# Attention with a forgetting decay, then a gated FFN, on one core: rows of q and k filled by DMA instead of cleaned on GpSimd, other load times, and a last output summed piece by piece

## The chip, the cores and the metric

The kernel runs on one core of one Trainium2 chip. The metric is the time of one execution in microseconds (us) as the device measures it. The engines are named as in the profile: PE is TensorE's matmul, PEld its weight load, DVE is VectorE, ACT is ScalarE, POOL is GpSimd, and SP is SyncE, which in this kernel only issues DMAs.

## The reference

Two stages, one behind the other. The first is causal attention whose scores carry a decay from a running sum over log f; the second is an FFN with a convolution over three neighbours and a gate. There are 8 batches, 8 heads, 576 positions, a head width of 64, 512 model columns and 1024 FFN columns.

```
scores = scale * np.matmul(q, k.transpose(0, 1, 3, 2))
log_f = np.log(np.clip(f, 0.0001, 1.0))
cum = np.cumsum(log_f, axis=-1)
decay = cum[:, :, :, None] - cum[:, :, None, :]
scores = np.where(causal, -1000000000.0, scores + decay)
attn = softmax(scores)
x = heads side by side of np.matmul(attn, v)
...
h = np.maximum(x @ w_in, 0.0)
conv_out += conv_w[k][None, None, :] * hp[:, k:k + S, :]   # k = 0, 1, 2
gate = 1.0 / (1.0 + np.exp(-conv_out))
return h * gate @ w_out
```

## The kernel before

A **half batch** (hb, 0 to 15) is four heads of one batch; a **block** (b, 0 to 7) is one batch, so two half batches and then the FFN of their 576 rows.

q and k are loaded by transposing DMAs (`load_qk`, four ring buffers `stq` and `stk`) that see the 64 float32 of a head as 128 16-bit columns. Afterwards the odd partitions of a buffer hold the upper halves, which are used as bfloat16, and the even partitions hold the lower halves, which are of no use. `clamp` therefore multiplies the even partitions by zero and sets a constant there where it is needed (two instructions for each side of a half batch, 1152 columns each). `rows_of` then overwrites one even row of q and two of k with the cumulated log f (in DRAM as `kd`), so that the score matmul adds the decay by itself. For half batch 0 the decay comes from extra matmuls on `sel_k` and `sel_q`.

The scores of a half batch come in groups: the tail (the last 64 positions), the diagonal tiles and the tiles off the diagonal. ACT takes their exponentials; POOL zeroes what lies above the diagonal in the diagonal tiles and the tail (`diag_mask`, `tail_mask`, by affine_select). When a block's eight heads are there, PE sums the columns (`sums`), DVE turns and inverts the sums (`recip`, L376 and L377, once in a block) and spreads them (`spread`, L380), PE multiplies by v (`pv`), and DVE scales the result into `xt` (`norm`, L389).

The FFN of a block has eight pieces (ff) of 128 columns: `ffn1` on PE, `relu` on ACT, two scalar_tensor_tensor on DVE for the convolution (L409, L411), `tanh` on ACT, and one more on DVE for the gate (L418), into `hg`. Only when all eight are there does `ffn2` run, for five row groups of the output, each with one chain of eight matmuls over ff; ACT copies the result out and SP stores it.

What stands where on an engine is decided by a list scheduler in plain Python (`Plan`): each task has engines with a cost, predecessors, a key and buffers that it takes and gives. The order that comes out is the order in each engine's queue; at run time each engine works through its own queue and waits only for semaphores. Before the change the clamps of half batches 1 and 2 may go to POOL or DVE, all later ones go to POOL, and `rows_of` is issued from POOL:

```
cl.append(add({"POOL": 1.35, "DVE": 0.6} if hb < 3 else {"POOL": 1.35}, [t_ld[hb, s]], base - 1.0 + 0.1 * (2 * p + s),
...
t_rows[hb] = add({"POOL": 1.1}, cl, base - 0.8, lambda me, hb=hb: rows_of(hb), lag=2.5)
```

v comes as float32 by SP and is cast to float16 by POOL or DVE (L224, L226); the weights are loaded with a cast by DMAs from POOL.

## Time and profile before

| | |
|---|---|
| three runs | 332.43, 333.64 and 336.59 us; median 333.64 us |
| the profiled execution | 335.01 us, its span 333.3 us |
| mean granted TensorE clock | 0.923 |
| busy in the span | PE 78%, DVE 84%, ACT 60%, POOL 55% |

The span runs from the first instruction to the last; 1.7 us of the profiled execution lie outside it. A busy share is a mean over stages: the first third waits for loads, the last fifth has no loads left. A DVE or POOL instruction counts as busy from its start to its end, however much of that it stood still.

### The profile page before, as it was taken

How to read it: one execution, taken by the hardware profiler on the slowest of the kernel's cores; microseconds unless marked ns; L12 is line 12 of the kernel's file. 1: busy time of each engine (PE TensorE's matmuls, PEld its weight loads, DVE VectorE, ACT ScalarE, POOL GpSimd, SP SyncE). 2: the span in 40 equal slices, each digit the busy share in tenths (PEclk: the TensorE clock that was granted, in tenths of full speed). 3: DMA queues.
4: the chain of work that ended last, by engine and by line, in shares of the span. 5: the costliest groups of instructions: out<-in, count | busy, mean ns of one | idle time of the engine just before them, and what ended most of it. 6: DMA issues, size and time to landing. Idle time of an engine off the chain costs nothing.

```text
span 333.3 us, 6984 instructions
## 1 busy us (share of the span) xinstructions
PE 259.6 (78%) x2832; PEld 177.3 (53%) x2832; DVE 279.2 (84%) x319; ACT 201.0 (60%) x267; POOL 184.8 (55%) x193
## 2 busy tenths in 40 slices
...
GB/s 174 232 195 194 196 198 195 197 133 221 220 177 104 94 218 96 120 65 223 149 140 63 83 177 181 2 65 151 73 4 63 76 9 63 66 18 0 128 16 142
DMA packets 126182, 40.97 MB, mean 123 GB/s; under 512 B 118693, under 2 KB 121893, under 8 KB 126150
## 3 DMA queue, kind: packets, MB, share of 16 engines
q1 hardware_dynamic: 118592, 37.76, 53.3%
...
q10 hardware_dynamic: 326, 0.45, 0.5%
...
q14 instruction: 10, 0.08, 0.1%
...
## 4 chain that ended last, share of the span: by engine, by line
DVE 38%; PE 35%; SPq 11%; issue 5%; DMA 4%; ACT 4%; POOL 2%; DVEq 0%; POOLq 0%; ACTq 0%
PE ps L425 13%; DVE hg L418 10%; DVE u L409 9%; PE ps L399 9%; SPq L196 8%; DVE u L411 8%; PE ps L366 7%; PE ps L305 5%; DVE va L224 3%; DMA vf<-in_v_dram 3%; DVE xt L389 3%; SPq L218 3%; DVE rb L380 2%; DVE va L226 1%; DMA stk<-kd 1%
## 5 line engine op out<-in xcount | busy, mean ns | idle before, releaser
L305 PE MATMUL ps<-stq,stk 128*128 128x128 bf16 (+3 forms) x576 | 64.7, 254 | 31.5 <-DVE stq L202 10.6
L399 PE MATMUL ps<-xt,w_in_f 128*128 128x288 f16 x512 | 77.5, 303 | 13.3 <-ACT ht L403 8.5
L414 ACT ACTIVATE hg<-u,cw 128x576 f16<-128x576 f32 x64 | 49.5, 776 | 62.2 <-DVE u L411 62.0
L425 PE MATMUL ps<-w_out_f,hg 128*128 128x512 f16 x256 | 66.7, 415 | 21.0 <-DVE hg L418 17.3
L418 DVE SCALAR_TENSOR_TENSOR hg<-hg,ht 128x576 f16<-128x576 f16 x64 | 67.1, 1057 | 9.1 <-ACT hg L414 8.9
L332 ACT ACTIVATE pp<-ps 128x1024 f16<-128x1024 f32 x64 | 64.1, 1022 | 12.2 <-PE ps L305 10.1
L409 DVE SCALAR_TENSOR_TENSOR u<-ht,cwt 128x576 f32<-128x576 f16 x64 | 67.5, 1066 | 4.4 <-ACT ht L403 4.4
L399 PEld LDWEIGHTS <-w_in_f 128*128 128x128 f16 x512 | 51.6, 103 | 33.6 <-issue 14.7
L411 DVE SCALAR_TENSOR_TENSOR u<-ht,cwt,u 128x576 f32<-128x576 f16 x64 | 65.7, 1037 | 0.8
L305 PEld LDWEIGHTS <-stk 128*128 128x128 bf16 x576 | 41.5, 104 | 44.3 <-issue 12.6
L345 POOL TENSOR_SCALAR_AFFINE_SELECT pp<-pd 128x1024 f16<-128x1024 f32 x32 | 39.6, 1236 | 33.8 <-ACT pd L342 33.1
L425 PEld LDWEIGHTS <-hg 128*128 128x128 f16 x256 | 26.3, 105 | 55.2 <-DVE hg L418 20.0
L202 POOL TENSOR_SCALAR stk<-stk,lim 128x1152 uint16<-128x1152 uint16 x29 | 50.5, 1744 | 0.5 <-DMA stk<-in_k_dram 0.5
L202 POOL TENSOR_SCALAR stq<-stq,lim 128x1152 uint16<-128x1152 uint16 x28 | 46.1, 1646 | 4.9 <-DMA stq<-in_q_dram 2.8
L403 ACT ACTIVATE ht<-ps 128x576 f16<-128x576 f32 x64 | 41.0, 651 | 12.4 <-PE ps L399 12.1
L320 POOL TENSOR_SCALAR_AFFINE_SELECT pt<-p 128x256 f16<-128x256 f32 x16 | 11.0, 689 | 60.1 <-ACT p L317 60.1
L342 ACT ACTIVATE pd<-ps 128x1024 f32<-128x1024 f32 x32 | 32.7, 1023 | 3.8 <-PE ps L305 2.1
L366 PE MATMUL ps<-pp,ones_h 128*64 128x128 f16 (+3 forms) x576 | 28.6, 249 | 1.0 <-POOL pp L345 0.6
L438 ACT COPY ob<-ps 128x1024 f32<-128x1024 f32 (+1 forms) x24 | 19.1, 796 | 14.7 <-PE ps L425 13.5
L366 PEld LDWEIGHTS <-ones_h 128*64 128x64 f16 x640 | 24.0, 116 | 7.0 <-issue 4.3
L366 PE MATMUL ps<-pp,va 128*64 128x128 f16 (+3 forms) x576 | 25.5, 241 | 2.6 <-DVE xt L389 2.6
L366 PEld LDWEIGHTS <-va 128*64 128x64 f16 x640 | 22.6, 111 | 6.7 <-issue 4.8
...
## 6 DMA issues: line engine op xcount, KB each, us to landing
...
stq<-in_q_dram SPq DMA_TRANSPOSE x17, 5.9
```

Of the source, the lines that this page charges most:

```text
L202: eng.tensor_scalar(t, t, lim[:, 2 * side:2 * side + 1], lim[:, 2 * side + 1:2 * side + 2], op0=ALU.mult, op1=ALU.add)
L305: nc.tensor.matmul(o, tk[:, h * S + k0:h * S + k0 + 128], tq[:, h * S + q0:h * S + q0 + n], start=True, stop=hb > 0)
L332: nc.scalar.activation(pp_t[slot[t_dg, "p"]][:, 1024 * s:1024 * (s + 1)], ps_t[slot[t_sc, "ps"]], AF.Exp, scale=SCALE)
L345: nc.gpsimd.affine_select(pp_t[slot[t_dg, "p"]][:, 2048:3072].rearrange("p (m j) -> p m j", j=128), pd_t[slot[t_ex, "pd"]].rearrange("p (m ...
L366: nc.tensor.matmul(ps[64 * s:64 * (s + 1), AB + q0:AB + q0 + n], left_of(s, h, m), p, start=first and x in (0, 3), stop=last and x in (2, ...
L399: nc.tensor.matmul(ps[:, MB + 288 * a:MB + 288 * (a + 1)], w_in_f16[:, cc, 128 * ff:128 * (ff + 1)], xt[:, cc, 288 * a:288 * (a + 1)], sta ...
L403: nc.scalar.activation(ht_t[slot[t_m1, "ht"]][:, 1:1 + S], ps_t[slot[t_m1, "ps"]][:, MB:MB + S], AF.Relu, scale=0.5)
L409: nc.vector.scalar_tensor_tensor(u, ht[:, 0:S], cwt[:, ff, 0:1], ht[:, 1:1 + S], op0=ALU.mult, op1=ALU.add)
L411: nc.vector.scalar_tensor_tensor(u, ht[:, 2:2 + S], cwt[:, ff, 1:2], u, op0=ALU.mult, op1=ALU.add)
L414: nc.scalar.activation(hg_t[slot[t_g0, "hg"]][:, ff, :], u_t[slot[t_u, "u"]], AF.Tanh, scale=cw[:, ff, 1:2])
L418: nc.vector.scalar_tensor_tensor(hv, hv, 1.0, ht_t[slot[t_m1, "ht"]][:, 1:1 + S], op0=ALU.add, op1=ALU.mult)
L425: nc.tensor.matmul(o, hg[:, ff, 128 * c:128 * (c + 1)], w_out_f16[:, ff, :], start=(ff == 0), stop=(ff == NFF - 1))
```

## The change

1. **Rows by DMA.** From half batch 4 on nothing is cleaned. `fill` writes all 64 even partitions by two DMAs a side from SP: 60 rows of zeros (`blank`, DRAM) and 4 rows from `kq` or `kk`, DRAM tiles that hold the cumulated log f and the constants. Each fill waits for the transposing DMA of its side.
2. **First half batches.** Half batches 1 to 3 (`NCL = 4`) are still clamped, all on DVE, and `rows_of` is issued from SP.
3. **Constants.** Three memsets on POOL at the start and six DMAs from POOL behind the first mask write `kq`, `kk` and `blank`.
4. **Load times.** The keys of the q and k loads and of v change, v is loaded a head at a time (still five DMAs), and pairs of weight pieces wait for later masks.
5. **Last output.** In block 7 `ffn2_last` adds each ff into three open sums as soon as its gate is there, and ACT or DVE copies them out. In block 6 the five groups get nearly the same key.

```
+    kq = dpool.tile([4, BH, S], BF16, name="kq")
+    kk = dpool.tile([4, BH, S], BF16, name="kk")
+    blank = dpool.tile([60, HS], BF16, name="blank")
...
+    def fill(hb, side):
+        t, width = ((stq_t, HS), (stk_t, HS + 64))[side]
+        t = t[hb % RING]
+        c = slice(hb * HH, (hb + 1) * HH)
+        nc.sync.dma_start(even_rows(t, width, 8, 60), blank)
+        nc.sync.dma_start(even_rows(t, width, 0, 4), (kq, kk)[side][:, c, :].rearrange("j h s -> j (h s)"))
...
+    nc.gpsimd.memset(stk_t[3], 0.0)
+    nc.gpsimd.memset(stq_t[3][0:BH, 0:S], 1.0)
+    nc.gpsimd.memset(stq_t[3][0:BH, S:2 * S], -1.0)
     nc.gpsimd.iota(lii[:, 0:1], pattern=[[0, 1]], base=0, channel_multiplier=1)
...
+    def ffn2_last(t_o, g0, ff, a):
...
+            if a < 2:
+                c = 2 * a + j
+                nc.tensor.matmul(ps[:, 512 * j:512 * (j + 1)], hg[:, ff, 128 * c:128 * (c + 1)], w_out_f16[:, ff, :],
+                                 start=(ff == 0), stop=(ff == NFF - 1))
...
-                t_ld[hb, s] = add({"SP": 2.4}, old, base - 5.0 + 0.1 * s,
+                t_ld[hb, s] = add({"SP": 2.4}, old, base - 2.2 + 0.1 * s,
...
-        t_vl[hb] = add({"SP": 2.5}, [], base - 3.5, lambda me, hb=hb: load_v(hb, me, nc.sync), take=["vf"], lag=2.0,
+        t_vl[hb] = add({"SP": 2.5}, [], 4 * b + 2.4 + 0.1 * (hb % 2), lambda me, hb=hb: load_v(hb, me, nc.sync), take=["vf"], lag=2.0,
...
-            for p in range(2):
+            for p in range(2 if hb < NCL else 0):
                 for s in range(2):
-                    cl.append(add({"POOL": 1.35, "DVE": 0.6} if hb < 3 else {"POOL": 1.35}, [t_ld[hb, s]], base - 1.0 + 0.1 * (2 * p + s),
...
+                    cl.append(add({"DVE": 0.6}, [t_ld[hb, s]], base - 1.0 + 0.1 * (2 * p + s),
...
+            fl = [add({"SP": 1.1}, cl, base - 0.8, lambda me, hb=hb: rows_of(hb), lag=2.3)] if cl else [add({"SP": 1.1}, [t_ld[hb, s], t_const], base - 1.5 + 0.1 * s, lambda me, hb=hb, s=s: fill(hb, s), lag=2.3, dma=0.9)
+                  for s in range(2)]
```

How the queues change is seen at two places. On POOL in the middle of the program (half batches 10 and 11), before; L202 is the clamp, L208 and L210 the rows, L320 and L345 the masks, L224 and L226 the casts of v:

```order
L202 TENSOR_SCALAR stq2_86<-stq2_86,lim_76 128x1152 x2
L202 TENSOR_SCALAR stk2_90<-stk2_90,lim_76 128x1152 x2
L208 DMA stq2_86<-kd_65 1x16x144
L210 DMA stk2_90<-kd_65 2x2304
L320 AFFINE_SELECT pt0_105<-p30_111 128x256
L345 AFFINE_SELECT pp4_103<-pd0_109 128x1024
L202 TENSOR_SCALAR stq3_87<-stq3_87,lim_76 128x1152
L224 CAST va2_97<-vf1_93 128x4x256
L226 CAST va2_97<-vf1_93 64x4x64
L202 TENSOR_SCALAR stk3_91<-stk3_91,lim_76 128x1152
```

The same part of POOL's queue in the changed kernel, where masks are L335 and L360 and casts L235 and L237:

```order
L360 AFFINE_SELECT pp0_101<-pd0_111 128x1024
L235 CAST va2_99<-vf0_94 128x4x256
L237 CAST va2_99<-vf0_94 64x4x64
L360 AFFINE_SELECT pp1_102<-pd1_112 128x1024
L235 CAST va3_100<-vf1_95 128x4x256
L335 AFFINE_SELECT pt3_110<-p31_114 128x256
L360 AFFINE_SELECT pp2_103<-pd0_111 128x1024
L360 AFFINE_SELECT pp3_104<-pd1_112 128x1024
L237 CAST va0_97<-vf2_96 64x4x64
L335 AFFINE_SELECT pt0_107<-p30_113 128x256
```

No clamp and no DMA is left there; masks and casts are all that POOL has from the weights on.

On SP at the loads of half batches 3 and 4, before; L196 is the transposing load, L218 the load of v:

```order
L196 DMA_TRANSPOSE stq3_87<-in_q_dram 128x2304
L196 DMA_TRANSPOSE stk3_91<-in_k_dram 128x2304
L218 DMA vf0_92<-in_v_dram 128x4x64 x4
L218 DMA vf0_92<-in_v_dram 64x4x64
L196 DMA_TRANSPOSE stq0_84<-in_q_dram 128x2304
L196 DMA_TRANSPOSE stk0_88<-in_k_dram 128x2304
```

In the changed kernel (L199 transposes, L220 and L221 are the rows of half batch 3, L227 and L229 load v, L215 and L216 are the fill of half batch 4):

```order
L199 DMA_TRANSPOSE stq0_86<-in_q_dram 128x2304
L199 DMA_TRANSPOSE stk0_90<-in_k_dram 128x2304
L220 DMA stq3_89<-kq_65 1x2304
L221 DMA stk3_93<-kk_66 2x2304
L227 DMA vf2_96<-in_v_dram 128x4x64 x4
L229 DMA vf2_96<-in_v_dram 64x4x64
L227 DMA vf0_94<-in_v_dram 128x4x64 x4
L229 DMA vf0_94<-in_v_dram 64x4x64
L215 DMA stq0_86<-blank_67 60x2304
L216 DMA stq0_86<-kq_65 4x2304
L215 DMA stk0_90<-blank_67 60x2304
L216 DMA stk0_90<-kk_66 4x2304
```

Rows and fills stand in SP's queue, behind the loads of v; further on output stores stand between them too.

## Rows read from the trace of the kernel before

**Rows 1.** The page: busy time of the engines, and the chain that ended last.

```profile
PE 259.6 (78%) x2832; PEld 177.3 (53%) x2832; DVE 279.2 (84%) x319; ACT 201.0 (60%) x267; POOL 184.8 (55%) x193
...
DVE 38%; PE 35%; SPq 11%; issue 5%; DMA 4%; ACT 4%; POOL 2%; DVEq 0%; POOLq 0%; ACTq 0%
```

**Rows 2.** Groups by line and shape: xcount, busy us, mean ns, idle before.

```profile
L409 DVE SCALAR_TENSOR_TENSOR u<-ht,cwt 128x576 f32<-128x576 f16 x64 | 67.5, 1066 | 4.4 <-ACT ht L403 4.4
L418 DVE SCALAR_TENSOR_TENSOR hg<-hg,ht 128x576 f16<-128x576 f16 x64 | 67.1, 1057 | 9.1 <-ACT hg L414 8.9
...
L411 DVE SCALAR_TENSOR_TENSOR u<-ht,cwt,u 128x576 f32<-128x576 f16 x64 | 65.7, 1037 | 0.8
...
L202 POOL TENSOR_SCALAR stk<-stk,lim 128x1152 uint16<-128x1152 uint16 x29 | 50.5, 1744 | 0.5 <-DMA stk<-in_k_dram 0.5
...
L271 POOL MEMSET ones_h<- 128x256 f16 x1 | 0.3, 301 | 0.0
```

**Rows 3.** Timeline, 128.5 to 134 us, DVE, then POOL: start us, us.

```profile
128.65 7.19 DVE L418 SCALAR_TENSOR_TENSOR hg<-hg,ht 128x576 f16<-128x576 f16 x1
...
130.07 2.59 POOL L202 TENSOR_SCALAR stq<-stq,lim 128x1152 uint16<-128x1152 uint16 x2
132.65 2.57 POOL L202 TENSOR_SCALAR stk<-stk,lim 128x1152 uint16<-128x1152 uint16 x2
```

**Rows 4.** Timeline of DVE: `recip` of block 1 and of block 7.

```profile
66.01 0.78 DVE L376 STREAM_TRANSPOSE st<-ps 128x576 f32<-128x576 f32 x1 [7.16 <-PE ps L366]
...
291.73 0.78 DVE L376 STREAM_TRANSPOSE st<-ps 128x576 f32<-128x576 f32 x1 [0.84 <-PE ps L366]
```

**Rows 5.** Timeline ahead of block 1's `recip`: PE, then POOL.

```profile
64.10 0.40 PE L305 MATMUL ps<-stq,stk 128*128 128x64 bf16 x4 [6.98 <-DMA stk<-kd]
...
60.26 0.52 POOL L210 DMA_DIRECT2D stk<-kd  x1
```

**Rows 6.** Windows: span, then busy (instructions) of each engine, clock, DMA share, GB/s.

```profile
225.00:300.00 75.00, 68.83 (x870) 49.19 (x868) 69.45 (x88) 54.17 (x76) 24.36 (x21) 1.00 0.22 58
300.00:315.00 15.00, 15.00 (x94) 8.88 (x92) 14.48 (x21) 10.60 (x16) 0.00 (x0) 0.89 0.10 36
```

**Rows 7.** The chain at 279.9 to 291 us: start us, us, what.

```profile
281.70 0.98 PE ps L399 x8
282.68 0.88 PE ps L305 x12
283.56 1.73 PE ps L425 x8
...
286.70 2.21 PE ps L366 x60
...
290.00 0.99 PE ps L430 x16
```

**Rows 8.** Timeline at 275 us: DVE, then POOL.

```profile
275.12 0.81 DVE L411 SCALAR_TENSOR_TENSOR u<-ht,cwt,u 128x576 f32<-128x576 f16 x1
275.85 1.64 DVE L409 SCALAR_TENSOR_TENSOR u<-ht,cwt 128x576 f32<-128x576 f16 x1
...
275.39 1.49 POOL L345 TENSOR_SCALAR_AFFINE_SELECT pp<-pd 128x1024 f16<-128x1024 f32 x1 [2.58 <-ACT pd L342]
```

**Rows 9.** Timeline of SP's queue: a load of q, four of five DMAs of a v load.

```profile
149.58 2.90 SPq L196 DMA_TRANSPOSE stq<-in_q_dram  x1
...
158.10 2.05 SPq L218 DMA_DIRECT2D vf<-in_v_dram  x4
```

**Rows 10.** DMA queues and issues: share of 16 engines; median us to landing.

```profile
q1 hardware_dynamic: 118592, 37.76, 53.3%
...
stq<-in_q_dram SPq DMA_TRANSPOSE x17, 5.9
```

**Rows 11.** Timeline of the end, 320 to 333.3 us: PE, then SP.

```profile
320.86 7.07 PE L425 MATMUL ps<-w_out_f,hg 128*128 128x512 f16 x25 [0.54 <-DVE hg L418]
...
329.52 1.28 SPq L449 DMA_DIRECT2D out_dram<-ob  x2
```

More of the change, by code (lines that the diff above doesn't have):

```diff
@@ L142 @@
     RING, NP, NPT, NVA, NVF, NHT, NU, NOB = 4, 6, 4, 4, 3, 4, 3, 3
+    NCL = 4
     AB = 256
@@ L215, in load_v @@
         base = int(v.offset) + hb * HH * S * D
-        for kb in range(NKB):
-            n = 128 if kb < NKB - 1 else SL
-            eng.dma_start(vf[0:n, :, kb, :],
-                          bass.AP(tensor=v.tensor, offset=base + kb * 128 * D, ap=[[D, n], [S * D, HH], [1, D]]))
+        for h in range(HH):
+            eng.dma_start(vf[:, h, 0:4, :],
+                          bass.AP(tensor=v.tensor, offset=base + h * S * D, ap=[[D, 128], [128 * D, 4], [1, D]]))
+        eng.dma_start(vf[0:SL, :, 4, :],
+                      bass.AP(tensor=v.tensor, offset=base + 512 * D, ap=[[D, SL], [S * D, HH], [1, D]]))
     def cast_v(t_load, t_cast, part, eng):
@@ L261 @@
                                    op0=ALU.mult, op1=ALU.subtract)
-    for t in range(RING):
+    for t in range(RING - 1):
         nc.gpsimd.memset(stk_t[t][:, HS:HS + 64], 0.0)
@@ L267 @@
     clamp(0, 1, 0, nc.vector)
-    nc.scalar.dma_start(kd[0], kc[0:BH])
-    nc.scalar.dma_start(kd[1], kc[BH:128])
+    nc.scalar.dma_start(kq[0], kc[0:BH])
+    nc.scalar.dma_start(kk[1], kc[0:BH])
+    nc.scalar.dma_start(kk[2], kc[BH:128])
     nc.scalar.dma_start(cwrow, moe_conv_w)
@@ L449, in store, with constants @@
                 nc.sync.dma_start(outf[r:r + SL, 256 * a:256 * (a + 1)], ob[64 * a:64 * (a + 1), 0, 0:256])
+    def constants():
+        for j in (1, 2):
+            nc.gpsimd.dma_start(kq[j], stq_t[3][0:BH, 0:S])
+        nc.gpsimd.dma_start(kk[0], stq_t[3][0:BH, S:2 * S])
+        for t in (kq, kk):
+            nc.gpsimd.dma_start(t[3], stk_t[3][0:BH, 0:S])
+        nc.gpsimd.dma_start(blank, stk_t[3][0:60, 0:HS])
     add = plan.add
@@ L463, in weights @@
         for w in range(pieces):
-            made.append(add({"POOL": 0.9}, after, key + 0.1 * w,
+            made.append(add({"POOL": 0.9}, [after[w]], key + 0.1 * w,
                             lambda me, w=w: nc.gpsimd.dma_start(
```

49 lines of the change are left out of this document (37 added, 12 removed).

## The prediction

> **What bounds the kernel now.** I read the page first: DVE is the busiest engine with 84% of the span, and the chain that ended last runs over DVE for 38% and over PE for 35% [rows 1]. The reader should not take that as "DVE has 279 us of work". The groups by line show why: the three FFN instructions of DVE (L409, L411, L418) come 64 times each and take 67.5 + 65.7 + 67.1 = 200.3 us, a mean of 1.04 us [rows 2], while one of them that nobody disturbs takes 0.81 us [rows 8]. 192 x 0.81 = 155.5, so about 45 us of DVE's busy time is standing still. The timeline says where: at 128.65 one gate instruction lasts 7.19 us, and it ends when POOL's four clamps in a row (2.59 + 2.57 us) end [rows 3]. There are some such stretches in every block that still has clamps, and the clamps are slow in turn: 1.74 us in the mean against 1.29 us in that row [rows 2, 3].
>
> Then I cut the span in three at `recip`, which runs once in a block. Block 1's is at 66.0 us, block 7's at 291.7 us [rows 4]. So: 66.0 us up to block 1, 225.7 us for the six blocks behind it (37.6 us each), and 333.3 - 291.7 = 41.6 us from block 7's sums to the end. Each of the three has its own limit, and the change acts on all of them.
>
> **The clamps (main term): the six blocks.** From half batch 4 on POOL's clamps and its row DMAs go; what stays on it are masks and casts (the order shows no other row there). What is late next is either PE or DVE, so I work out both for one block.
>
> PE at the full clock, by groups of the chain [rows 7]: `ffn1` 64 matmuls, 8 x 0.98 = 7.84 us; `ffn2` 32, 4 x 1.73 = 6.92, and 0.99 for the last 64 rows; `sums` and `pv` 160, 2.21 / 60 x 160 = 5.89; scores 72, 0.88 / 12 x 72 = 5.28. Sum 26.9 us. In 225 to 300 us, where the clock is 1.00 and clamps are few, PE is busy 68.83 of 75 us, 91.8% [rows 6]: 26.9 / 0.918 = 29.3 us.
>
> DVE: 24 FFN instructions and 10 for `recip`, `spread` and `norm`, 34 in all. Where POOL does nothing, 21 instructions take 14.48 us, 0.69 us each [rows 6]: 23.4 us. To this come the masks and casts. A large mask that meets an FFN instruction holds it up by 1.64 - 0.81 = 0.83 us [rows 8]; there are four in a block, and 24 of DVE's 34 instructions are of that sort, so 4 x 0.83 x 0.7 = 2.3 us. The six short ones (two tail masks, four cast pieces) I set at half of that each, 1.7 us; this is an estimate. Sum 27.4 us, and at the 92.6% that DVE reaches in the same window (69.45 of 75 us) [rows 6], 29.6 us.
>
> Two engines that are both nearly full also wait for each other, so I take half a us more than the larger one: **30.1 us a block**, 6 x 30.1 = 180.6 us instead of 225.7. The saving of 45.1 us is, worked out from another side, the 45 us that DVE stood still. Bounds: 27.7 us if PE ran at 97%, and the rivals' figures below.
>
> **Up to block 1.** PE waits 6.98 us at 64.1 us for the rows of half batch 4, which POOL issued only at 60.26 us, behind clamps and a cast [rows 5]; the last sums of block 1 stand behind that. In the changed queue of SP the fill of half batch 4 stands behind two loads of v. Those cost 2 x 2.05 x 5 / 4 = 5.1 us of issue [rows 9] from about the time when half batch 3's rows go out, so I expect the fill some 7 us earlier, and the wait goes: 66.0 - 7.0 = 59.0 us. The bounds are 66.0 (v and the fill are late) and 57.
>
> The rest of this stage I cost at nothing, with its cover: nine more clamps on DVE at 0.69 us are 6.2 us, and DVE sits idle 7.16 us ahead of block 1's `recip` [rows 4]; without that cover they cost their 6.2. The six DMAs of the constants take 6 x 0.52 = 3.1 us of POOL [rows 5] between the first two masks, where block 0's sums wait for the scores of half batch 1 anyway; without it, 3.1. The memsets of 2368 + 2 x 576 columns stand ahead of the index instructions that DVE's first columns need. At 301 ns for 256 columns [rows 2] they take up to 4.1 us, but the first loads are still on their way then: 0 to 1 us, and I take 0. Weights and v come later than before but ahead of their users in PE's queue: 0.
>
> **The fills** are 24 sides of 64 rows x 4608 bytes = 0.295 MB. The trace has no such DMA. The hardware queue moved 37.76 MB in 53.3% of the span, 177.6 us of all engines [rows 10], or 0.213 MB a us, so a fill costs at most 1.39 us of the DMA engines and 33.3 us in all (longer packets make that less; nothing makes it negative). 177.6 + 33.3 = 211 us is 26.4 us a block, below 30.1 but not by much: the cover is thin, and if it is gone a block takes what SP and the DMAs need (rival B). On SP a fill adds two issues of about 0.52 us [rows 9].
>
> **The end.** Now PE starts 25 matmuls of `ffn2` at 320.86, when the last gate is done, and the last store is issued at 329.52 [rows 11]; from there to 333.3 are 3.8 us. From gate to end: 12.4 us. Changed: for the last ff four long matmuls (4 x 1.73 / 8 = 0.9) and two short ones (0.1), the copies on ACT and DVE side by side (1.0, an estimate), the store as now (3.8): 5.8 us. The seven earlier ff fit in PE's gaps, which DVE's pace leaves open. Saving 6.6 us: 41.6 becomes 35.0. Bounds: 2 us, if ACT does both large copies one after the other and the stores queue up, and 8 us.
>
> **Sum.** 59.0 + 180.6 + 35.0 = 274.6 us of span, plus the 1.7 us outside it 276.3; the profiled execution stood 1.4 us above the median, so I expect a median of **275 us**, 18% less.
>
> **Rivals.**
> A. *POOL's masks and casts hold DVE each time.* If all ten POOL instructions of a block cost DVE 0.83 us, it needs 23.4 + 8.3 = 31.7, at 92.6% 34.2 us a block: 59.0 + 205.4 + 35.0 + 0.3 = 300 us. For it: the row at 275 us. Against it: at 92.6% DVE already includes some of these, and masks that fall on `spread` and `norm` need not disturb. The Trainium skill ("SBUF — State Buffer", Who interferes with whom) says that a VectorE instruction with two SBUF inputs and a GpSimd instruction that reads SBUF exclude each other, and that the later one waits for the whole of the other. The row at 275 us agrees: the mask took 1.49 us and the DVE instruction beside it 1.64 [rows 8].
> B. *SP becomes the bound.* In one block SP issues four loads (4 x 2.90), two loads of v (5.1), eight fills (4.1) and stores (about 2.6), 23.4 us by [rows 9, 11]. A fill must wait until its load has landed, 5.9 us [rows 10], and everything behind it in the queue waits too. If one such landing in each half batch isn't covered by the next load's issue, a block takes 23.4 + 11.8 = 35.2 us: 306 us. Against it: in the order the loads of the next half batch mostly stand between a load and its fill.
> C. *Slower than before.* The same wait at all four loads, because fills stand directly behind their loads or behind stores that wait for ACT: 23.4 + 23.6 = 47 us a block, 376 us. It decides above 41 us a block (59 + 6 x 41 + 35.3 = 340), so from three bare landings in four on. I saw few such places in the order, but the later loads leave less lead than before.
> D. *The clamps were not what held DVE.* Then the blocks keep 37.6 us and only the ends gain: 59 + 225.7 + 35.3 = 320 us, or 327 if the early wait stays as well. Against it: the end of the 7.19 us coincides with the clamps' end.
>
> **Chances and range.** Forecast (28.5 to 31.5 us a block, 265 to 284 us) 0.58; quicker 0.06; A 0.16; B 0.08; D 0.06; C 0.06. The range takes the forecast, the quick side as far as PE at 97% allows (59 + 166.2 + 35.3 = 261) and A: **262 to 300 us**. Two per cent is about what a measurement of this kernel can tell from no change, 327 to 340 us: faster has the forecast, the quick side, A, B and half of D, 0.91; within it the other half of D and a third of C, 0.05; slower 0.04.
>
> **What would show it.** Right: in the groups by line L424, L426 and L433 (the same three instructions) fall to 0.80 to 0.90 us in the mean and none lasts over 2.5 us; `recip` of block 1 near 59 us and 30 us between blocks; PE busy over 90% from 60 us on; at most 6 us from the last gate to the end. Wrong: PE waiting for `stk<-blank` or `stk<-kk` for over 1 us in most blocks (B, C); DVE instructions of 1.6 us beside most masks (A); long DVE instructions with no clamp beside them (D). What would hurt the forecast most is a fill that lands later than I think, since it stands in a queue that waits in order.

## The result, and the profile after

The changed kernel takes 304.12 us (median of four runs, 301.16 to 304.39) against 334.01 us: a ratio of 0.908, with a 95% interval of 0.900 to 0.916. The prediction was 275 us, 262 to 300. So 9% were gained where 18% were forecast, and the time lies just outside the range. The profiled execution has a span of 302.7 us. Executions of one kernel differ by up to 5% and fall into a fast and a slower group: medians and intervals below use the fast ones, with their number beside them, and a star marks a profile of a slower one.

The page of the changed kernel, the lines of [rows 1]: busy time of the engines, and the chain that ended last.

```profile
PE 249.2 (82%) x2832; PEld 172.2 (57%) x2832; DVE 232.2 (77%) x323; ACT 198.1 (65%) x266; POOL 97.8 (32%) x120
...
PE 38%; DVE 25%; SPq 12%; DMA 10%; ACT 7%; issue 6%; DVEq 0%; ACTq 0%
```

Its three FFN groups on DVE, the lines of [rows 2]: xcount, busy us, mean ns, idle before.

```profile
L433 DVE SCALAR_TENSOR_TENSOR hg<-hg,ht 128x576 f16<-128x576 f16 x64 | 54.6, 858 | 15.4 <-ACT hg L429 15.1
...
L424 DVE SCALAR_TENSOR_TENSOR u<-ht,cwt 128x576 f32<-128x576 f16 x64 | 54.9, 870 | 6.0 <-ACT ht L418 6.0
L426 DVE SCALAR_TENSOR_TENSOR u<-ht,cwt,u 128x576 f32<-128x576 f16 x64 | 58.4, 919 | 0.9
```

DVE's instructions run nearly as forecast: 167.9 us instead of 200.3, 0.87 us in the mean (forecast 0.80 to 0.90; L426 is just above). What is new stands in the chain: SP's queue and DMA make 22% of it (15% before). The windows show where. They are cut at `recip` of each block, and a block's stretch ends at its own `recip` (first line: up to block 0; last line: behind block 7). Each line gives span, busy us of PE, PEld, DVE, ACT and POOL, granted clock, DMA share (above 1 where the times of packets on an engine overlap), GB/s.

```profile
0.00:39.23 39.23, 22.82 (x245) 17.31 (x246) 13.47 (x40) 16.35 (x19) 20.32 (x54) 0.91 0.92 181
39.23:71.39 32.16, 22.67 (x297) 17.57 (x296) 25.17 (x37) 20.07 (x28) 10.54 (x11) 0.89 1.33 180
71.39:104.33 32.94, 28.16 (x322) 19.26 (x321) 26.23 (x37) 23.85 (x32) 13.50 (x9) 0.95 0.98 196
104.33:143.19 38.86, 31.49 (x364) 21.43 (x363) 27.54 (x37) 23.64 (x33) 14.73 (x11) 0.91 1.00 210
143.19:175.14 31.95, 27.32 (x326) 19.01 (x326) 28.61 (x37) 24.97 (x34) 14.45 (x12) 1.00 0.92 209
175.14:204.42 29.28, 28.32 (x346) 20.02 (x345) 27.45 (x36) 24.25 (x34) 9.25 (x11) 1.00 0.94 211
204.42:233.69 29.27, 28.31 (x346) 20.00 (x345) 27.44 (x36) 24.24 (x34) 9.24 (x11) 1.00 0.58 151
233.69:262.70 29.01, 28.53 (x349) 20.18 (x348) 26.70 (x36) 23.84 (x34) 5.73 (x6) 1.00 0.12 43
262.70:302.70 40.00, 31.59 (x248) 17.46 (x246) 29.58 (x41) 16.94 (x25) 0.00 (x0) 0.94 0.18 63
```

Blocks 5 to 7 take 29.2 us each with PE busy for 28.3 us or more of it: the pace that was forecast (30.1), and a little better. The blocks before are longer: in them PE stands, the DMA share is 0.92 or more, and up to block 3 the granted clock is below 1. A high DMA share alone does not make a block long, since block 5 has 0.94. Against the sum of the prediction: up to block 1's `recip` 71.4 us instead of 59.0 (12.4 more), the six blocks 191.3 instead of 180.6 (10.7 more), the end 40.0 instead of 35.0 (5.0 more). Together these are the 28.1 us by which the span misses 274.6. Three places show how.

**The start.** Timeline of ACT and then of PE in the changed kernel, 9 to 24 us: start us, us, what, idle before it and who ended that.

```profile
9.53 0.51 ACTq L282 DMA_DIRECT2D kq<-kc  x1
12.12 0.47 ACTq L283 DMA_DIRECT2D kk<-kc  x1
17.36 0.51 ACTq L284 DMA_DIRECT2D kk<-kc  x1
20.52 0.64 ACTq L285 DMA_DIRECT2D cwrow<-in_moe_conv_w_dram  x1
21.21 0.38 ACT L332 ACTIVATE p<-ps 128x256 f32<-128x256 f32 x1 [12.79 <-DMA vf<-in_v_dram]
...
23.10 0.98 PE L301 MATMUL ps<-ident,cwrow 3*128 3x3 f32 x8 [5.13 <-DMA cwrow<-in_moe_conv_w_dram]
```

The first exponential stands behind four DMA issues in ACT's own queue, which come at intervals of 3 to 5 us; it runs at 21.2 us (15.5 in the kernel before), although its scores are there from 13 us on. The change put a third table DMA there.

**The rows of half batch 3.** PE ahead of block 1's `recip`, POOL's DMAs of w_out, and on SP the two loads of v and the first fill of half batch 4, in the changed kernel:

```profile
58.94 2.08 PE L320 MATMUL ps<-stq,stk 128*128 128x64 bf16 x16 [6.19 <-DMA stk<-kk]
...
43.97 3.53 POOL L500 DMA_DIRECT2D w_out_f<-in_moe_w_out_dram  x4
...
52.07 5.14 SPq L227 DMA_DIRECT2D vf<-in_v_dram  x4
57.26 1.88 SPq L229 DMA_DIRECT2D vf<-in_v_dram  x1
59.19 2.30 SPq L227 DMA_DIRECT2D vf<-in_v_dram  x4
...
62.27 0.91 SPq L215 DMA_DIRECT2D stq<-blank  x1
```

The same DMA in the kernel before, the first of its four:

```profile
97.18 0.91 POOL L465 DMA_DIRECT2D w_out_f<-in_moe_w_out_dram  x1
```

The 6.98 us of [rows 5] are not gone; 6.19 us of the same kind stand one half batch earlier. And w_out does not come later: a POOL without clamps gets to these DMAs 53 us sooner, right among the loads of the first blocks. Two of the four pieces of w_in move in the same way, from 74 and 96 us to 35 and 39. SP's issues are slow in this stretch: the two loads of v take 10.2 us (52.07 to 62.23) where 5.1 were forecast, and the fill of half batch 4 goes out at 62.3 us, behind the 60.26 of [rows 5] and not 7 us ahead of it.

**The casts of v.** DVE, ACT and PE in block 3:

```profile
119.34 1.52 DVE L237 CAST va<-vf 64x256 f16<-64x256 f32 x1 [5.41 <-DMA vf<-in_v_dram]
...
121.62 0.78 ACT L429 ACTIVATE hg<-u,cw 128x576 f16<-128x576 f32 x1 [6.26 <-DVE u L426]
122.30 1.00 ACT L357 ACTIVATE pd<-ps 128x1024 f32<-128x1024 f32 x1
...
123.35 5.40 PE L440 MATMUL ps<-w_out_f,hg 128*128 128x512 f16 x16 [6.46 <-ACT pd L357]
```

This is one chain: v lands late, a small cast in DVE's queue waits for it, the convolution behind the cast waits, then tanh (L429), then the exponential behind tanh in ACT's queue (L357), which frees the PSUM buffer that `ffn2` waits for. The 16 matmuls after the wait take 5.40 us; at the full clock they are 2 x 1.73 = 3.46 [rows 7]. The granted clock from 123.35 to 128.75 us is 0.66. So this wait cost 6.5 + 1.9 us, most of what block 3 has above 29.2.

### The profile page after: what moved, and what is told of

Read it like the earlier page. It is cut to its first block, busy times and chain, and to the rows that moved or that the text cites. A ratio compares the mean times of both kernels' runs of the same rounds, so it can differ in the third digit from the quotient of the medians.

```text
span 302.7 us, 6950 instructions
## 1 busy us (share of the span) xinstructions
PE 249.2 (82%) x2832; PEld 172.2 (57%) x2832; DVE 232.2 (77%) x323; ACT 198.1 (65%) x266; POOL 97.8 (32%) x120
## 2 busy tenths in 40 slices
DMA packets 127551, 48.59 MB, mean 161 GB/s; under 512 B 118344, under 2 KB 121608, under 8 KB 127520
## 3 DMA queue, kind: packets, MB, share of 16 engines
q1 hardware_dynamic: 120602, 44.88, 68.7%
## 4 chain that ended last, share of the span: by engine, by line
PE 38%; DVE 25%; SPq 12%; DMA 10%; ACT 7%; issue 6%; DVEq 0%; ACTq 0%
PE ps L440 12%; PE ps L414 9%; SPq L199 8%; PE ps L381 7%; DVE u L426 6%; DVE hg L433 5%; DVE u L424 5%; PE ps L320 4%; DMA vf<-in_v_dram 4%; DMA stq<-in_q_dram 3%; DVE xt L404 3%; PE ps L454 2%; DMA stk<-kk 2%; ACT pd L357 2%; DVE rb L395 2%
## 5 line engine op out<-in xcount | busy, mean ns | idle before, releaser
L320 PE MATMUL ps<-stq,stk 128*128 128x128 bf16 (+3 forms) x576 | 63.6, 247 | 22.2 <-DVE stq L205 10.9
L414 PE MATMUL ps<-xt,w_in_f 128*128 128x288 f16 x512 | 73.8, 292 | 6.2 <-DVE xt L404 2.8
L429 ACT ACTIVATE hg<-u,cw 128x576 f16<-128x576 f32 x64 | 49.6, 778 | 31.8 <-DVE u L426 31.5
L433 DVE SCALAR_TENSOR_TENSOR hg<-hg,ht 128x576 f16<-128x576 f16 x64 | 54.6, 858 | 15.4 <-ACT hg L429 15.1
L360 POOL TENSOR_SCALAR_AFFINE_SELECT pp<-pd 128x1024 f16<-128x1024 f32 x32 | 44.7, 1398 | 66.0 <-ACT pd L357 66.0
L440 PE MATMUL ps<-w_out_f,hg 128*128 128x512 f16 x224 | 55.3, 398 | 10.5 <-ACT pd L357 7.6
L424 DVE SCALAR_TENSOR_TENSOR u<-ht,cwt 128x576 f32<-128x576 f16 x64 | 54.9, 870 | 6.0 <-ACT ht L418 6.0
L426 DVE SCALAR_TENSOR_TENSOR u<-ht,cwt,u 128x576 f32<-128x576 f16 x64 | 58.4, 919 | 0.9
L320 PEld LDWEIGHTS <-stk 128*128 128x128 bf16 x576 | 39.6, 101 | 34.1 <-issue 13.8
L440 PEld LDWEIGHTS <-hg 128*128 128x128 f16 x224 | 22.5, 101 | 36.9 <-issue 12.3
L357 ACT ACTIVATE pd<-ps 128x1024 f32<-128x1024 f32 x32 | 32.7, 1023 | 1.1 <-PE ps L325 1.0
L335 POOL TENSOR_SCALAR_AFFINE_SELECT pt<-p 128x256 f16<-128x256 f32 x16 | 13.8, 862 | 50.8 <-ACT p L332 50.8
L235 POOL CAST va<-vf 128x1024 f16<-128x1024 f32 x12 | 15.7, 1312 | 36.6 <-DMA vf<-in_v_dram 30.7
L395 DVE STREAM_TRANSPOSE rb<-rt 128x576 f32<-128x576 f32 x32 | 22.7, 746 | 0.0
L404 DVE TENSOR_TENSOR xt<-ps,rb 128x576 f16<-128x576 f32 x32 | 22.1, 726 | 0.0
(75 smaller groups left out, 160.6 us busy)
```

What stands on the lines that cost most here:

```text
L320: nc.tensor.matmul(o, tk[:, h * S + k0:h * S + k0 + 128], tq[:, h * S + q0:h * S + q0 + n], start=True, stop=hb > 0)
L357: nc.scalar.activation(pd_t[slot[me, "pd"]], ps_t[slot[t_dg, "ps"]], AF.Exp, scale=SCALE)
L360: nc.gpsimd.affine_select(pp_t[slot[t_dg, "p"]][:, 2048:3072].rearrange("p (m j) -> p m j", j=128), pd_t[slot[t_ex, "pd"]].rearrange("p (m ...
L414: nc.tensor.matmul(ps[:, MB + 288 * a:MB + 288 * (a + 1)], w_in_f16[:, cc, 128 * ff:128 * (ff + 1)], xt[:, cc, 288 * a:288 * (a + 1)], sta ...
L424: nc.vector.scalar_tensor_tensor(u, ht[:, 0:S], cwt[:, ff, 0:1], ht[:, 1:1 + S], op0=ALU.mult, op1=ALU.add)
L426: nc.vector.scalar_tensor_tensor(u, ht[:, 2:2 + S], cwt[:, ff, 1:2], u, op0=ALU.mult, op1=ALU.add)
```

## The experiments

In the table the stretches are those of the one profiled execution (block 0 and 1: time of `recip`; then blocks 2 to 4, blocks 5 to 7, and the end). How far such a stretch can be trusted is seen at e_combo1 and e_combo_b6: their queues are the same up to 92 us, and their first two `recip` differ by 1.4 and 2.1 us. Where no interval is given, the total is not compared.

| kernel | median us (executions) | ratio to before (95%) | block 0, 1 | 2 to 4 | 5 to 7 | end |
|---|---|---|---|---|---|---|
| before | 334.0 (4) | 1 | 35.5, 66.0 | 125.6 | 100.1 | 41.6 |
| changed | 304.1 (4 of 4) | 0.908 (0.900-0.916) | 39.2, 71.4 | 103.7 | 87.6 | 40.0 |
| b_dveclamp | 301.5 (4 of 4) | 0.900 (0.895-0.905) | 42.1, 73.8 | 94.7 | 88.3 | 40.1 |
| e_dveclamp | 303.6 (4 of 4) | 0.906 (0.902-0.911) | 38.1, 73.6 | 97.9 | 89.6 | 40.0 |
| e_start* | 295.2 (1 of 4) | - | 34.5, 70.0 | 103.1 | 87.5 | 40.2 |
| e_castpool* | 293.1 (1 of 4) | - | 40.0, 72.4 | 97.2 | 88.5 | 39.6 |
| e_combo1 | 292.4 (3 of 4) | 0.871 (0.867-0.875) | 33.3, 65.8 | 97.7 | 88.2 | 38.8 |
| e_oldload* | 298.7 (3 of 4) | 0.889 (0.883-0.895) | 37.0, 70.6 | 101.2 | 87.2 | 39.9 |
| e_v32 | 300.3 (3 of 4) | 0.894 (0.882-0.906) | 38.8, 74.3 | 98.4 | 87.6 | 38.3 |
| e_combo_v32 | 292.3 (4 of 4) | 0.872 (0.868-0.877) | 37.0, 66.9 | 98.1 | 87.6 | 40.5 |
| e_vpool | 311.1 (3 of 4) | 0.925 (0.919-0.932) | 38.7, 73.8 | 107.5 | 88.4 | 39.7 |
| e_combo_dve | 294.9 (4 of 6) | 0.880 (0.875-0.885) | 32.4, 66.4 | 96.0 | 89.6 | 40.5 |
| e_wlate* | 305.7 (3 of 6) | 0.909 (0.904-0.914) | 39.1, 71.6 | 106.8 | 87.6 | 39.9 |
| e_combo_wlate* | 292.3 (1 of 6) | - | 37.3, 65.4 | 107.4 | 87.9 | 40.3 |
| e_combo_dve_wlate | 294.4 (2 of 6) | 0.876 (0.872-0.881) | 33.1, 69.1 | 95.4 | 89.6 | 38.8 |
| e_combo_nov | 283.7 (4 of 4) | 0.848 (0.842-0.855) | 37.7, 65.5 | 89.2 | 87.6 | 38.6 |
| e_combo_nowout | 287.5 (3 of 4) | 0.857 (0.849-0.865) | 33.9, 61.8 | 93.5 | 88.1 | 40.1 |
| e_combo_nov_nowout | 279.3 (2 of 4) | 0.834 (0.824-0.844) | 33.6, 61.6 | 88.2 | 87.6 | 38.6 |
| e_oldtail | 301.7 (3 of 4) | 0.902 (0.894-0.909) | 39.4, 72.1 | 98.9 | 87.0 | 42.0 |
| e_combo_b6 | 293.5 (5 of 6) | 0.873 (0.869-0.878) | 34.7, 67.9 | 97.1 | 88.2 | 38.8 |

**Which part gained: the clamps.** b_dveclamp edits the kernel before:

```
-cl.append(add({"POOL": 1.35, "DVE": 0.6} if hb < 3 else {"POOL": 1.35}, [t_ld[hb, s]], ...
+cl.append(add({"DVE": 0.6}, [t_ld[hb, s]], ...          # clamp(hb, p, s, nc.vector)
```

> Edit, on the kernel before the change: all clamps on VectorE instead of POOL, nothing else (rows still by DMA from POOL, old loads, old last output, no fills). It puts some 52 clamps of about 0.58 us on DVE, 30 us in all. Theory (POOL's clamps were what held DVE): the three FFN instructions of DVE fall from a mean of 1.04 to 0.88 us or less, the six blocks from block 1 to block 7 take 30 to 32 us each instead of 37.6, total 295 to 305 us. Rival D of the prediction (the clamps were not what held DVE): the blocks keep 37 us or get longer by the clamps, total 327 us or more.

e_dveclamp edits the changed kernel: `NCL = 16`.

> Edit: NCL = 16, so no fills at all; every half batch is cleaned on VectorE and its three rows come by two small DMAs from SP. It puts 48 clamps of about 0.58 us more on DVE (28 us, 3.5 us a block) and takes 24 fills (some 24 us of the DMA engines, about 20 us of SP's issue) away. Theory: the last three blocks, 29.2 us each and with DVE at 0.94, go to 32 to 33 us, the blocks before gain 1 to 2 us each from the lighter queue, total 302 to 310 us. Rival (the fills are what holds the first five blocks): blocks 2 to 4 at 31 us or less, total below 298 us.

Moving the clamps from one engine to the other, in the kernel before, gains as much as the whole change (the intervals overlap). The FFN groups of b_dveclamp, and POOL's first DMAs of w_out there:

```profile
L409 DVE SCALAR_TENSOR_TENSOR u<-ht,cwt 128x576 f32<-128x576 f16 x64 | 56.9, 902 | 0.0
L411 DVE SCALAR_TENSOR_TENSOR u<-ht,cwt,u 128x576 f32<-128x576 f16 x64 | 53.7, 850 | 0.2
L418 DVE SCALAR_TENSOR_TENSOR hg<-hg,ht 128x576 f16<-128x576 f16 x64 | 50.0, 790 | 5.2 <-ACT hg L414 5.2
...
46.98 2.67 POOL L465 DMA_DIRECT2D w_out_f<-in_moe_w_out_dram  x3
```

They are 160.6 us instead of 200.3, and the 64 clamps, now all on DVE (57 came from POOL), cost 43.6 us: DVE's total falls from 279.2 to 250.6 us. Rival D is out. The run shows a price, too: with the clamps gone from POOL and nothing else changed, w_out's DMAs run at 47 us instead of 97, and block 1's `recip` comes at 73.8 us instead of 66.0. And the fills are worth nothing in sum in the changed kernel: with them (304.1) and without (303.6) it is the same. Without fills blocks 5 to 7 are 0.7 us longer each, not the 3 to 4 that were expected, and blocks 2 to 4 are 1.9 us shorter each.

**The start and the casts.** e_start, the last lines of the set-up:

```
-    nc.scalar.dma_start(kq[0], kc[0:BH])     # and kk[1], kk[2], cwrow
     make_identity(nc, ident)
+    nc.gpsimd.dma_start(cwrow, moe_conv_w)   # and kq[0], kk[1], kk[2]
```

> Edit: the three DMAs that write the cumulated log f and the one that loads the convolution weights are issued from POOL behind its constants instead of from ACT; all other queues stay as they are. Theory 1 (start): in the changed kernel ACT's queue stands at these four issues from 9.5 to 21.2 us, so the first exponential comes at 21.2 instead of about 12 us, and the convolution weights come late for PE (5.1 us of waiting at 23.1). Here the first exponential at about 12 to 14 us, recip of block 0 at 34 instead of 39.2, recip of block 1 at 64 to 67 instead of 71.4, total 297 to 300 us. Rival (the DMA engines set the pace up to 210 us): the first exponential comes earlier, but recip of block 1 moves by less than 2 us and the total stays within 2 us of 304.

e_castpool, in both cast tasks:

```
-    lambda e, me, hb=hb: cast_v(t_vl[hb], me, 0, e)
+    lambda e, me, hb=hb: cast_v(t_vl[hb], me, 0, nc.gpsimd)
```

> Edit: the nine casts of v that the planner put on VectorE are issued on POOL at the same place of the order; every other queue keeps its order. Theory 2 (v late): v is now loaded behind the fills, DVE's casts wait 5.4 and 3.5 us for it in blocks 3 and 4 and hold the gates, and PE waits 6.5 us at 123.4 us for them. Here these waits go from DVE to POOL, block 3 shrinks from 38.9 us to 32 to 34, total 297 to 300 us. Rival (the wait only moves: POOL's masks then stand behind the casts that wait for v): blocks 2 to 4 as long as before or longer, total 303 to 310 us.

e_combo1 has both edits.

> Edit: the start of e_start and the casts of e_castpool together. If the two losses are independent (about 3 and 5 us against the changed kernel's 304.1), the total is 294 to 296 us. Theory (the start is hidden behind the rows of half batch 3, which SP's queue brings late in either case: recip of block 1 moved only from 71.4 to 70.0 us with the earlier start): total 297 to 299 us, PE still waits 6 to 8 us at about 58 us.

e_start brings the first exponential to 12.9 us and block 0's `recip` forward by 4.7 us, as expected, but block 1's by 1.4 only: PE then waits 7.9 us for half batch 3 instead of 6.2, so on block 1 the rival was right. e_castpool takes block 3 from 38.9 to 31.0 us. So the late v on DVE was block 3's loss. In e_castpool it is POOL that waits for v, 10.3 us ahead of one cast in block 3, and this costs less. Neither edit alone has an interval, so whether the two gains add is open. Together they are clear: e_combo1's interval lies below that of the changed kernel, and of the versions that compute the whole reference none is faster beyond the noise. In its run the wait for half batch 3 was 5.4 us.

**What the early blocks wait for.** e_oldload undoes the keys of the loads:

```
-                t_ld[hb, s] = add({"SP": 2.4}, old, base - 2.2 + 0.1 * s,
+                t_ld[hb, s] = add({"SP": 2.4}, old, base - 5.0 + 0.1 * s,
-        t_vl[hb] = add({"SP": 2.5}, [], 4 * b + 2.4 + 0.1 * (hb % 2), ...
+        t_vl[hb] = add({"SP": 2.5}, [], base - 3.5, ...
```

> Edit: the old keys of the loads of q, k and v (item 4 undone, but for the form of the v load and the weights); fills, constants and the last output stay. Theory 2 (v late): v comes ahead of the fills again, no cast of v waits over 1 us, block 3 takes 31 to 33 us instead of 38.9; block 1's recip comes later by up to 5 us since the rows of half batch 3 stand behind more loads; total 297 to 302 us. Rival (the later loads are what makes the fills fit): fills land late in most blocks, PE waits over 1 us for them in blocks 2 to 5, total above 308 us.

It takes 298.7 us and its interval lies below that of the changed kernel: the new keys were a loss of some 5 us. Block 3 takes 30.8 us there, block 2 38.9.

e_v32 and e_combo_v32 (that is e_combo1 with it) load less of v; e_vpool issues v elsewhere:

```
-            eng.dma_start(vf[:, h, 0:4, :], ... ap=[[D, 128], [128 * D, 4], [1, D]]))
+            eng.dma_start(vf[0:n, h, 0:4, :], ... ap=[[D, n], [128 * D, 4], [1, D]]))   # n = 32 from half batch 3 on
...
-    lambda me, hb=hb: load_v(hb, me, nc.sync)       # e_vpool
+    lambda me, hb=hb: load_v(hb, me, nc.gpsimd)
```

> Edit: from half batch 3 on the four large DMAs of each v load fetch 32 of 128 partitions (the others keep an older v, so the output is not the reference's); the number of DMAs, their places and all waits stay. It takes about 13 x 1536 packets of 256 bytes, some 27 us, off the DMA engines and nothing off the queues' orders. Theory 3 (DMA engines full): up to 210 us the DMA share is 0.92 to 0.99, and that sets blocks 2 to 4; here those blocks (32.9, 38.9, 31.9 us) come down to about 30 each and the total to 288 to 294 us. Rival (SP's queue works in order, and its waits and issue times set the pace whatever the bytes): blocks 2 to 4 stay above 33 us in the mean, total 300 us or more.

> Edit: e_combo1, and from half batch 3 on the four large DMAs of each v load fetch 32 of 128 partitions (so the output is not the reference's): 27 us less for the DMA engines at the same queue orders. Theory 3 (DMA engines full): blocks 1 to 4 take 29.5 to 30.5 us instead of 32.5, total 281 to 285 us. Rival (SP's queue, issuing for 0.94 of the time up to 210 us, is the limit whatever the bytes): those blocks stay at 32 us or more, total 290 to 294 us.

> Edit: the 80 DMAs that load v are issued from POOL instead of SP, at the same places of the order; bytes, waits and all other queues stay. Theory 5 (SP's queue is the bound of the first 210 us): in the changed kernel SP issues DMAs for 0.92 to 0.96 of every 30 us from 30 to 210 us, 208 us in all, 54 us of it for v. Here SP is done with its loads some 45 us earlier, PE's wait for the rows of half batch 3 (6.2 us at 58.9 us) falls below 3 us, blocks 1 to 4 take 30 to 31 us each, and the total is 283 to 290 us. Rival (the DMA engines are the bound, and they move the same bytes): SP finishes earlier by less than 15 us, total 298 to 304 us.

e_combo_dve is e_combo1 with `NCL = 16`.

> Edit: e_combo1 with NCL = 16, so every half batch is cleaned on VectorE and there are no fills. Theory 3 (the DMA engines set blocks 1 to 4, at 32.5 us each in e_combo1, and the fills are 24 us of their work): these blocks come down to 30 to 31 us, the last ones go from 29.3 to 30.3 us, total 284 to 288 us against 292.7. Rival (the fills cost less than the clamps that they replace): total 292 to 296 us.

Theory 3 in this form fell. e_v32 has 300.3 us where 288 to 294 were expected. In e_combo_v32 the hardware queue took 62.0% of 293.1 us, 181.7 instead of 211.6 us in e_combo1, and the time is the same. In e_combo_dve the load of the DMA engines is lighter still and blocks 2 to 4 gain only 0.6 us each in the mean (block 2 loses 4.2, blocks 3 and 4 gain 3.1 and 2.7), which the last blocks and the end give back; with fills the kernel is about 1% faster there (0.871 against 0.880, the intervals touch). Theory 5 fell too: in e_vpool SP no longer issues v, 54.0 us in the changed kernel, but its loads of q and k take 136.7 us to issue instead of 99.1, and it ends its last fill at 219.4 us, as the changed kernel does at 218.8. The DMA queues of e_vpool and of the changed kernel: packets, MB, share of 16 engines' span.

```profile
q1 hardware_dynamic: 82458, 35.44, 59.1%
q0 software_dynamic: 10096, 12.19, 22.2%
```

```profile
q1 hardware_dynamic: 120602, 44.88, 68.7%
q0 software_dynamic: 6512, 2.74, 7.5%
```

For the same 48.59 MB the packets took 81.3% of 309.4 us, 251.5 us, instead of 76.2% of 302.7, 230.7 us (230.7 to 242.1 in the nine kernels that move the same bytes with v on SP), and single loads stood in SP's queue for 9 us (a load of q at 33.66). The kernel is slower, 311.1 us. What part of that the packets cost was not told apart from v's late landing: a cast on DVE waits 8.0 us for it at 97 us. The Trainium skill ("Trainium Kernel Development and Optimization", Key Constraints) says that DMAs from SP, ACT and POOL run on the same 16 engines and that issuing from several only saves issue time. This run agrees in that nothing was gained, though SP issued for 14.4 us less in all.

**The weights.** In e_wlate, e_combo_wlate (e_combo1 with it) and e_combo_dve_wlate (e_combo_dve with it) the planner's order stays, and only the four DMAs are held back:

```
-    lambda me, w=w: nc.gpsimd.dma_start(...)
+    lambda me, w=w: (held.append if width == 128 else lambda d: d())(lambda: nc.gpsimd.dma_start(...))
-    lambda me, x=x, y=y: diag_mask(x, y),
+    lambda me, x=x, y=y, i=i: (diag_mask(x, y), [d() for d in held if i == 6]),
```

> Edit, on the changed kernel: the four DMAs of w_out are issued behind POOL's mask 6 (61.4 us) instead of behind mask 5 (44 us); all other rows of all queues stay. Theory 6 (weights too early): packets of w_out take 11.6 us of all DMA engines between 45 and 60 us, ahead of the rows of half batch 3; here PE's wait for these rows (6.2 us at 58.9 us) falls below 3 us, recip of block 1 comes at 65 to 68 us instead of 71.4, total 298 to 301 us; ffn2 of block 0 at 85 us still finds its weights. Rival (SP's issue times and the landing of the rows set it): recip of block 1 moves by less than 2 us, total 302 to 305 us.

> Edit: e_combo1 with the same four DMAs behind mask 6. Theory 6: recip of block 1 at 60 to 63 us instead of 65.8, total 286 to 290 us against 292.7. Rival: recip of block 1 moves by less than 2 us, total 291 to 294 us.

> Edit: e_combo_dve (no fills, all clamps on VectorE) with the same four DMAs behind mask 6. Theory 6: recip of block 1 at 61 to 64 us instead of 66.4, block 2 no longer 36 us but 31 to 33, total 288 to 292 us against 296.3. Rival: total 294 to 298 us.

PE's waits in e_wlate that correspond to the 6.19 us, first where it was and then the new one:

```profile
55.20 1.16 PE L320 MATMUL ps<-stq,stk 128*128 128x64 bf16 x16
...
88.94 2.08 PE L320 MATMUL ps<-stq,stk 128*128 128x64 bf16 x16 [7.57 <-DMA stk<-blank]
```

Half of theory 6 holds: the weights were what delayed half batch 3, whose wait is gone. The other half fell: block 1 is no earlier (71.6 us), since PE then waits 2.8 us for a mask that stands behind the four issues and a cast of v on POOL, the fills of half batch 5 now land 7.6 us late (3.6 in the changed kernel), and the kernel is no faster (305.7 us; the intervals overlap). e_combo_wlate's block 1 gains only 0.4 us, e_combo_dve_wlate's loses 2.7 and its total can't be told from e_combo_dve's (0.876 and 0.880). This later place was no better. So the last three runs left transfers out, and their outputs are not the reference's:

```
+        if hb > 2:                  # e_combo_nov, in load_v: no DMA of v from half batch 3 on
+            return
...
-    nc.gpsimd.dma_start(dst[...], src[...])          # e_combo_nowout, w_out only
+    nc.gpsimd.memset(dst[...], 0.03125)
```

> Edit: e_combo1 without the loads of v from half batch 3 on (older values stay, so the output is not the reference's); all other rows of all queues stay. It takes 13 x 2304 packets, some 40 us, off the DMA engines and 13 x 3.4 = 44 us off SP's issue. Theory 3b (the load phase as a whole, SP's queue and the DMA engines together, sets blocks 1 to 4): blocks 2 to 4 take 29 to 30.5 us instead of 32.0 to 33.2, total 283 to 287 us. Rival (these blocks are limited by the engines' own order, not by loads): total 290 us or more, as with the smaller v loads (292.3).

> Edit: e_combo1 with the four DMAs of w_out replaced by four memsets on POOL at the same place (constant weights, so the output is not the reference's). It takes 11.6 us off the DMA engines between 38 and 56 us and nothing off SP. Theory 7 (a sum, not a place: before block 3 each microsecond of the DMA engines costs the same wherever it stands): recip of block 1 at 62 to 63 us instead of 65.8 and no new wait behind it, total 286 to 289 us. Rival (SP's queue sets the pace): recip of block 1 within 1.5 us of 65.8, total 291 to 294 us.

> Edit: both of the last two. Theory 3b and 7: recip of block 1 at 62 us, all later blocks at 29 to 30 us, total 278 to 282 us, which is the prediction's pace for the blocks. Rival: total 288 us or more.

Windows of e_combo_nov_nowout at its `recip`s, blocks 1 to 4, columns as above:

```profile
33.56:61.59 28.03, 21.41 (x297) 16.75 (x296) 25.30 (x34) 20.10 (x28) 15.53 (x14) 1.00 1.10 188
61.59:89.83 28.24, 26.57 (x322) 18.72 (x321) 25.37 (x35) 23.29 (x32) 10.29 (x11) 1.00 0.89 205
89.83:118.54 28.71, 27.76 (x338) 19.55 (x337) 27.63 (x34) 23.71 (x34) 11.64 (x12) 1.00 0.85 197
118.54:149.82 31.28, 29.04 (x354) 20.41 (x353) 27.26 (x36) 24.93 (x35) 12.90 (x13) 1.00 0.69 147
```

SP's two loads of v and the first fill of half batch 4 in e_combo_nowout, then the longest wait of POOL for v in blocks 2 to 4 of e_combo1 and of e_combo_v32:

```profile
44.88 2.27 SPq L227 DMA_DIRECT2D vf<-in_v_dram  x4
...
47.95 2.19 SPq L227 DMA_DIRECT2D vf<-in_v_dram  x4
...
50.93 0.90 SPq L215 DMA_DIRECT2D stq<-blank  x1
```

```profile
135.69 1.04 POOL L235 CAST va<-vf 128x1024 f16<-128x1024 f32 x1 [12.07 <-DMA vf<-in_v_dram]
```

```profile
133.76 1.04 POOL L236 CAST va<-vf 128x1024 f16<-128x1024 f32 x1 [9.71 <-DMA vf<-in_v_dram]
```

Theory 7 and 3b hold in size: without w_out block 1's `recip` comes at 61.8 us, without v blocks 2 to 4 lose 8.5 us, with neither the kernel is nearly at the forecast pace and at 279.3 us. For w_out the mechanism is seen: without it the same two loads of v take 6.0 us to issue on SP, against 9.0 in e_combo1 and 10.2 in the changed kernel, and PE's wait for half batch 3 is gone. Moved behind mask 6 it gained nothing, which fits the sum of theory 7: up to block 2 each such transfer counts, wherever it stands.

For v the cause stays open. Fewer bytes of v alone gave nothing and no v at all gave 9 us, so it is not the bytes; SP's time to issue v hardly changed with them (50.8 us in e_combo_v32, 52.0 in e_combo1). But that time alone is not shown as the cause either: e_combo_dve saves as much of SP's issue time as e_combo_nov (173.4 and 168.9 us in all, of 210.6) and of the DMA engines' time (198.3 and 195.8 us, of 234.5), and gains 1.7 us in blocks 2 to 4 instead of 8.5, though its clamps load DVE beside it. A third possibility is the late landing itself: in blocks 2 to 4 POOL's casts wait 39.1 us for v in e_combo1 and 35.0 in e_combo_v32, with masks behind them in the queue, and in e_combo_nov they wait for no DMA. Issue time, place in the queue and this wait were not told apart. In e_combo_nowout PE also ran at a higher granted clock in blocks 2 and 3 (1.00 against 0.95). The constant data are not needed for that, since e_castpool has 1.00 in both blocks; what part of the gain is the clock was not tried.

**The end.** e_oldtail and e_combo_b6 (e_combo1 with it):

```
-        if b == B - 1:
+        if b == B:                                                # e_oldtail: never ffn2_last
-            key = k1 + 4.0 + (0.8 if b < B - 2 else 0.1) * c
+            key = k1 + 4.2 + 0.8 * c                              # both
```

> Edit: item 5 alone is undone: block 7 uses the old output path (all eight gates first, then five chains) and block 6 the old keys. Theory 4 (what the end gains is mostly given back ahead of the last gate): the time from block 7's recip to the end was 41.6 us in the kernel before and 40.0 in the changed one, so the total rises by only 1 to 3 us, and the last gate comes 2 to 3 us earlier after recip than with the change. Rival (the new end gains the 6.6 us that the prediction gave it, and something else ahead of it was lost): total 309 to 312 us.

> Edit: e_combo1 with block 6's keys of its last output as before the change (spread out instead of nearly equal). Theory 4 (in the end block 6's output stands in one piece of 8 us on PE ahead of block 7's ffn1, and DVE waits 2 to 3 us behind it): the last gate comes 29 us behind block 7's recip instead of 31.8, the stretch from recip to the end takes 36 to 37.5 us instead of 38.8, total 290.5 to 291.5 us. Rival (PE is full there in either order): the stretch stays within 0.5 us.

The second line does more than undo block 6: the change had moved the keys of every block's output by 0.2, and from 99 us on e_oldtail's queues differ from the changed kernel's (blocks 2 to 4 take 98.9 us instead of 103.7). So its median, which can't be told from the changed kernel's, does not price the end, and the last stretch does so roughly: 42.0 us without the new end and 40.0 with it, 2.0 us as theory 4 expected, but b_dveclamp with the old end has 40.1 and e_combo1 with the new one 38.8. Part of the spread is the clock: the last 25 matmuls of `ffn2` take 7.85 us in e_oldtail and 5.57 in b_dveclamp. The 6.6 us of the prediction are out in each pair. e_combo_b6 shows why so little is left: the last gate comes 28.7 us behind `recip` instead of 30.4 in e_combo1, and PE's last matmul ends 32.2 us behind it in both. PE of the changed kernel around its last gates:

```profile
274.93 7.07 PE L440 MATMUL ps<-w_out_f,hg 128*128 128x512 f16 x32
281.93 1.06 PE L445 MATMUL ps<-w_out_f,hg 128*64 128x256 f16 x16
282.92 3.11 PE L414 MATMUL ps<-xt,w_in_f 128*128 128x288 f16 x24
...
295.24 1.04 PE L454 MATMUL ps<-w_out_f,hg 128*128 128x512 f16 x4
296.21 0.30 PE L457 MATMUL ps<-w_out_f,hg 128*64 128x256 f16 x2
```

From 274.9 us to the end there is no gap ahead of these groups: PE is full, so the order of block 6's output on it does not matter.

## Why the prediction was wrong

- **The clamps (main term): right.** The three DVE groups have means of 0.86 to 0.92 us, PE is at 97% in blocks 5 to 7, and these take 29.2 us against 30.1. Rival D is refuted by b_dveclamp. (The 7.19 us instruction of [rows 3] ends 0.6 us behind the clamps and not with them; that is about the time it takes undisturbed.) The masks and casts, 4.0 us a block in the sum and 8.3 in rival A, cost the FFN instructions less: 167.9 - 155.5 = 12.4 us in eight blocks, 1.6 us each (2.0 by the medians of the three, 0.75, 0.81 and 0.82 us, since the 0.81 of the sum is too long for the gate). POOL's large masks take 1.40 us in the mean and 1.10 in the median and in a quiet stretch (39.7 us), so some of them wait, too. The Trainium skill ("SBUF — State Buffer", Who interferes with whom) says that of a VectorE instruction with two SBUF inputs and a GpSimd instruction that reads SBUF the one that comes first holds the shared ports and the other waits. The trace agrees in that both sides lengthen.
- **"59.0 up to block 1": this step failed, by 12.4 us.** It took the 6.98 us for gone. The wait moved one half batch ahead, since the rows of half batch 3 are behind the same transfers. Two terms were wrong and one was missing. "Weights and v come later than before but ahead of their users in PE's queue: 0" looked at keys, but w_out is in POOL's queue, and when the clamps left that queue its DMAs moved from 97 to 44 us; without them block 1 gains 4.0 us (e_combo_nowout). The 5.1 us for issuing two loads of v were 10.2, since SP's issues lengthen while other transfers run. And the DMAs at ACT's queue were not costed: the first exponential was 8.3 us later than in e_start, and block 0's `recip` 4.7. With w_out out and the start and the casts edited, block 1's `recip` is at 61.8 us; the 2.8 us to 59.0 stay open (half of w_in moved as well, and no run took it out).
- **"Six blocks of 30.1": right for three, too short for the others by 2 to 9 us, 10.7 in sum.** The 0 for v failed here: the late v held a cast on DVE in block 3 (7.9 us by e_castpool, and block 3 is as short with the old keys of e_oldload). The "thin cover" of the loads was named and put into rival B, with 35.2 us a block; the first three of the six took 34.6. So rival B's length was there in half the blocks, but hardly by its mechanism, the fills' landing: PE waits over 1 us for a fill once, 3.6 us in block 2. The price of a fill was about right: 68.7% of 302.7 against 58.5% of 301.1 us on the hardware queue (e_dveclamp) is 31.8 us for 24 fills, 1.33 us each, and between e_combo1 and e_combo_dve 1.47 (at most 1.39 forecast).
- **"35.0 at the end": mis-sized, 40.0.** "The seven earlier ff fit in PE's gaps" failed: PE had no gaps. From the last gate to the end it took 8.2 us instead of 5.8: PE 2.0 instead of 1.0, copies and hand-over 1.5 instead of 1.0, the last store 4.7 instead of 3.8. And the gate came 2.8 us later behind `recip` than before. Block 6's output, in one piece on PE ahead of it, is 1.7 us of that (e_combo_b6).
